# A gated linear attention and a feed-forward in one kernel: single chunks write their output transposed, by 32-column matmuls on quarters of the array

## The chip, the cores and the metric

The kernel runs on one core of a Trainium2 chip. The metric is the time on the device in microseconds (us), as the median of several runs. A profiled execution stands beside them; its span goes from the first to the last instruction.

## The reference

Two steps. A recurrent attention with a decay per feature (batch 4, 8 heads, 768 steps, head size 48), and then a feed-forward with a squared ReLU over all 3072 tokens (model width 384 = 8 x 48, inner width 2048):

```python
for t in range(S):
    state = alpha[:, :, t, :, None] * state + np.einsum('bhd,bhe->bhde', k[:, :, t], v[:, :, t])
    y[:, :, t] = np.einsum('bhd,bhde->bhe', q[:, :, t], state)
...
x = y.transpose(0, 2, 1, 3).reshape(B * S, H * D)
h = x @ w_in
r = np.maximum(h, 0.0)
g = r * r
return (g @ w_out).astype(np.float32)
```

## The kernel before

The recurrence is worked in chunks of 128 tokens, all 8 heads at once: 24 chunks (`NT`), 6 for each batch entry (`NCH`), so that chunks 0, 6, 12 and 18 begin a sequence and have no state to start from. Chunks 0 to 3 are worked as two "supers" of two chunks each (`add_super`); chunks 4 to 23 are "single" chunks (`add_chunk`, L401), of which 8 to 23 share the step of their scores in pairs (`PAIRS = 8`).

A single chunk goes through these steps:

- The logarithm of alpha on ScalarE (L411), its cumulative sum over the tokens as a matmul with a triangle (`e_p0`, L419), and the exponentials of the sum and of its negative (`e_A`, `e_Ai`, ScalarE). VectorE multiplies q and k by them (`e_qA`, L465, and `e_kI`, L472). GpSimd casts v to bf16 (`e_vb`, L414; the tile `vb`).
- TensorE transposes the scaled q and k, head pairs side by side in 128 rows with zeros as padding (`e_p1q`, `e_p1k`); a copy brings them to the tile `qkT` (`e_cp`).
- The scores k q^T of each head (`e_p2` in `add_scores`, L508): eight products a chunk on 64 of the 128 rows of the array, the two heads of a pair on different halves. VectorE masks them to the triangle (`e_sm`, L531; the tile `sm`, two halves `hh` of four heads each, called sm0 and sm1).
- The state: k^T v is added to `st` in PSUM (`e_ps`), VectorE decays it (`e_stm`), ScalarE copies it to bf16 (`e_sb`; the tile `sb`).
- The output (`add_back`, L545): y is the product of q with the state before the chunk (`e_p3a`, L576, four matmuls of 96 columns; a chunk that begins a sequence has none) plus the masked scores times v (`e_p3b`, L582, eight matmuls of 48 columns). The result has tokens on its rows.
- The tail (`add_tail`, L380): ScalarE copies y to the bf16 tile `xn`, TensorE transposes it in three parts (`e_p4`), and a copy on VectorE, or on ScalarE for early chunks, puts it into `xT_big` with features on the rows, as the feed-forward wants it.

The feed-forward runs over groups of chunks (4, 1, 1, and nine times 2): 16 tiles of the inner width times `w_in` (`add_moe1`), ReLU on ScalarE (L840), the square on VectorE (L848; the tile `gT`), and the product with `w_out` (`add_moe2`), whose result is copied to `ob` and stored.

The order of all instructions is laid out by a planner in the kernel's own code when the program is built (`Plan`, L61): each step is an `Op` with an engine (or several to choose from), a length, steps that it depends on, and a priority. Each engine then runs its instructions in exactly that order, and an instruction whose input is late holds up all that follow on its engine. Three of the planner's numbers bear on the change. `LEAD` (L330, used in `gate`) says how many chunks the cumulative sum of a chunk may be ahead of the feed-forward's progress. `PE_SLACK` and `PE_CALM` (L35, L36, used in `ready`) are the reserve that is planned between the end of another engine's step and the matmul that needs it: 0.05 us until the planned time of TensorE is at `PE_CALM`, and 0.25 us from there on. PSUM banks are slots, too: the attention's steps share two of them (`GLA_BANKS`), and a step that takes one gives it back when another step (`gives`) is done.

All matmuls are recorded under L254 (the helper `mm`), all transposes under L257, the copies of `cast` under L374 (ScalarE) and L376 (VectorE).

Of the kernel before, what the change touches and what calls it, by code (L numbers as in the profile page):

```python
# [8 lines left out]
FP32 = mybir.dt.float32  # L9
BF16 = mybir.dt.bfloat16  # L10
# [22 lines left out]

LAT = {"PE": 0.13, "ACT": 0.14, "DVE": 0.13, "POOL": 0.25}
PE_SLACK = 0.05  # L35
PE_CALM = 25.0  # L36
PAUSES = [(13.0, 1.0), (18.0, 1.0)]


# [17 lines left out]
def after(op, x=0.0):  # L57
    return (op, x)
# [88 lines left out]
def kernel(  # L147
# [10 lines left out]
    nc = tc.nc  # L158
    B, H, S, D = q.shape
    HD = H * D  # L160
    P = 128
    DP = 64
    NP = H // 2
    NCH = S // P
    d_model, d_ff = moe_w_in.shape
    n_tok = out.shape[0]
    KT = d_model // P
# [14 lines left out]
    big = ctx.enter_context(tc.tile_pool(name="big", bufs=1))  # L182
# [35 lines left out]
    for src, dst in ((utri_f, half_in), (sutri_f, half_ex)):  # L218
        nc.vector.memset(dst, 0.0)
        for ab in range(2):  # L220
            h = slice(ab * HF, ab * HF + HF)
            nc.vector.tensor_copy(dst[h, h], src[h, h])
    for ab in range(2):
        h = slice(ab * HF, ab * HF + HF)
# [10 lines left out]
    NBUF = 4  # L235
# [9 lines left out]
    nc.gpsimd.memset(kI_s[:, :, :, D:], 0.0)  # L245
    ae_s = big.tile([P, NBUF, 2, NP], FP32)
    nc.vector.memset(ae_s, 0.0)
    xT_big = big.tile([P, KT, n_tok], BF16)

    def pin(ins):  # L250
        tc.keep_in_program_order(ins)

    def mm(*a, **kw):
        pin(nc.tensor.matmul(*a, **kw))  # L254
# [4 lines left out]
    plan = Plan()  # L259
# [4 lines left out]
    GLA_BANKS = sl_bank[0:2]  # L264
# [4 lines left out]
    def psum(op, shape, dt):  # L269
        i = op.slot.bank  # L270
        return banks[i].tile(shape, dt, name=f"bank{i}")
# [6 lines left out]
    def add(eng, dur, emit, *deps, **kw):  # L278
        return plan.add(Op(eng, dur, emit, deps, **kw))
# [45 lines left out]
    C = [dict() for _ in range(NT)]  # L325
# [1 line left out]
    SRC = dict(srcs)  # L327
    EARLY = 2 * 3
    PAIRS = 8
    LEAD = 3.5  # L330

    NS = 2
    SIDE = 0
# [38 lines left out]
    def cast(op, out_t, in_t):  # L372
        if op.eng == "ACT":
            pin(nc.scalar.copy(out_t, in_t))  # L374
        elif op.eng == "DVE":
            pin(nc.vector.tensor_copy(out_t, in_t))  # L376
        else:
            pin(nc.gpsimd.tensor_copy(out_t, in_t))

    def add_tail(s, done, first, g):  # L380
        d = C[s]

        def e_xn():
            d["xn"] = work.tile([P, HD], BF16, name="xn")
            cast(xn, d["xn"], d["py"][:, 0:HD])
        xn = add("ACT", 0.36, e_xn, done, **g)
        first.gives = xn

        def e_p4():
            d["px"] = psum(p4, [P, KT, P], BF16)  # L390
            for j in range(KT):
                tr(d["px"][:, j, :], d["xn"][:, j * P:(j + 1) * P], ident_bf)
        p4 = plan.add(Op("PE", 0.165, e_p4, [xn], takes=GLA_BANKS, lat=0.14, **g))

        def e_xT():
            cast(xT, xT_big[:, :, s * P:(s + 1) * P], d["px"])
        xT = add({"ACT": 0.36, "DVE": 0.27} if s < EARLY else "DVE", 0.27, e_xT, p4, prio=-9.0)
        d["x"] = d["end"] = xT
        p4.gives = xT

    def add_chunk(s):  # L401
        d = C[s]
        b, c = divmod(s, NCH)
        i = s % NBUF
        L, qA, kI, ae = L_s[:, i], qA_s[:, i], kI_s[:, i], ae_s[:, i].rearrange("p j n -> p n j")
        old = C[s - NBUF].get("end") if s >= NBUF else None
        g = dict(prio=-10.0 + s * 0.01)
# [8 lines left out]
            pin(nc.gpsimd.tensor_copy(d["vb"], d["vt"]))  # L416
        vb = d["use_vt"] = add("POOL", 0.55, e_vb, d["ld_vt"], old, prio=-5.0)

        def e_p0():  # L419
            pm = d["pm"] = psum(p0, [P, 512], FP32)  # L420
            mm(pm[:, 0:HD], lhsT=utri_b[:, 0, :], rhs=L[:, :, 0:D], start=True, stop=True)
            for p in range(NP if s < TURN else 0):
                mm(pm[:, HD + p:HD + p + 1], lhsT=L[:, 2 * p:2 * p + 2, :], rhs=ones_col,
                   start=True, stop=True)
# [35 lines left out]
        else:  # L460
            p0.gives = ai
            ae1 = add("SPD", 0.4, e_aed, a_, lat=AE_LAT, **g)
# [12 lines left out]
        mk = d["use_kt"] = add("DVE", 0.47, e_kI, ai, d["ld_kt"], old, **g)  # L475
# [16 lines left out]
        if s < EARLY:  # L492
            cp = add({"ACT": 0.49, "DVE": 0.34}, 0, lambda: e_cp(0, NP), p1q, **g)
# [2 lines left out]
            cp = cpk = add("DVE", 0.61, lambda: e_cp(0, 2 * NP), p1k, **g)  # L496
        p1q.gives = cpk

        d.update(cps=[cp, cpk], mk=mk, vb_op=vb, ae1=ae1, kI=kI, ae=ae)
        if s < PAIRS:  # L500
            add_scores(s, 1)
            add_back(s)
        elif s % 2:
            add_scores(s - 1, 2)
            add_back(s - 1)
            add_back(s)

    def add_scores(s, n):  # L508
        pr = C[s:s + n]
# [32 lines left out]
        for hh, h in enumerate(hold):  # L542
            h.gives = pr[1]["sms"][hh]

    def add_back(s):  # L545
        d = C[s]
        b, c = divmod(s, NCH)
        g = dict(prio=-10.0 + s * 0.01)
        last = c == NCH - 1
        kI, ae, mk, vb, ae1 = d["kI"], d["ae"], d["mk"], d["vb_op"], d["ae1"]  # L550
        cp, (sm0, sm1) = d["cps"][0], d["sms"]

        if not last:
            def e_ps():
                if c == 0:
                    state["ps"] = ps_st.tile([P, NP, 2 * D], FP32, name="st")
                st = d["st"] = state["ps"]
                for p in range(NP):
                    mm(st[:, p, :], lhsT=kI[:, 2 * p:2 * p + 2, :], rhs=d["vb"][:, 2 * p:2 * p + 2, :],
                       start=(c == 0 and p == 0), stop=True, skip_group_check=True)  # L560
            prev = C[s - 1].get("sb") if s else None
            if c == 0 and s:
                prev = C[s - 2]["sb"]
            ps = plan.add(Op("PE", 0.17, e_ps, [mk, vb, ae1, prev], lat=0.16, **g))

            def e_stm():
                st4 = d["st"].rearrange("p n (j e) -> p n j e", j=2)
                pin(nc.vector.tensor_mul(st4, st4, bcast(ae, D)))  # L568
            stm = add("DVE", 0.47, e_stm, ps, ae1, prio=-2.0)

            def e_sb():
                d["sbt"] = work.tile([P, NP, 2 * D], BF16, name="sb")
                pin(nc.scalar.copy(d["sbt"], d["st"]))  # L573
            d["sb"] = add("ACT", 0.37, e_sb, stm, prio=-2.0)

        def e_p3a():  # L576
            d["py"] = psum(p3a, [P, 512], FP32)
            for p in range(NP):
                mm(d["py"][:, 2 * p * D:2 * (p + 1) * D], lhsT=d["qkT"][:, p, :], rhs=C[s - 1]["sbt"][:, p, :],
                   start=(p == 0), stop=False, skip_group_check=True)  # L580

        def e_p3b():  # L582
            if c == 0:
                d["py"] = psum(p3b, [P, 512], FP32)
            for hh in range(2):
                for p in range(NP):
                    h = 2 * p + hh
                    mm(d["py"][:, h * D:(h + 1) * D], lhsT=d["sm"][:, hh, p, :], rhs=d["vb"][:, h, :],
                       start=(c == 0 and hh == 0 and p == 0), stop=True, skip_group_check=True)
        p3a = None  # L590
        if c > 0:
            p3a = plan.add(Op("PE", 0.17, e_p3a, [cp, C[s - 1]["sb"], after(sm0)], takes=GLA_BANKS, **g))
        p3b = plan.add(Op("PE", 0.21, e_p3b, [after(sm1, 0.02), sm0, vb, after(p3a)], takes=None if c else GLA_BANKS, lat=0.15, **g))

        add_tail(s, p3b, p3a or p3b, g)

    def add_super(u):

# [424 lines left out]
```

## Time and profile before

| | us |
|---|---|
| median of 3 runs | 186.2 |
| lowest and highest of them | 185.51 and 186.7 |
| profiled execution | 185.78 |
| its span | 184.1 |

TensorE had the full clock granted throughout. The largest groups of the page, with the busy time of each (for matmuls, the mean of one includes the time through the array, and consecutive ones overlap):

| group | count | busy us | mean ns |
|---|---|---|---|
| TensorE, x times w_in, 256 columns | 480 | 61.1 | 273 |
| TensorE, g times w_out, 384 columns | 368 | 68.3 | 326 |
| TensorE, transposes of xn | 72 | 7.9 | 219 |
| TensorE, scores times v, 48 columns, single chunks | 160 | 7.4 | 183 |
| TensorE, q times state, 96 columns | 80 | 6.7 | 206 |
| ScalarE, ReLU | 96 | 56.1 | 602 |
| ScalarE, copy y to xn | 24 | 11.2 | 486 |
| VectorE, square | 96 | 42.8 | 470 |
| VectorE, mask of the scores, single chunks | 40 | 25.6 | 682 |
| VectorE, copy to xT_big | 19 | 6.7 | 354 |
| GpSimd, cast of v, single chunks | 20 | 10.8 | 542 |

How to read it: PE is TensorE, PEld its loads of weights, DVE is VectorE, ACT is ScalarE, POOL is GpSimd, SP is SyncE. In the page's name of a group, what stands before the arrow is written and what stands behind it is read; `64*128` means that 64 rows and 128 columns of the array were in use. The chain of waits is the work that ended last, followed back from the end.

### The profile page before, as it was taken

How to read it: one execution, taken by the hardware profiler on the slowest of the kernel's cores; microseconds unless marked ns; L12 is line 12 of the kernel's file. 1: busy time of each engine (PE TensorE's matmuls, PEld its weight loads, DVE VectorE, ACT ScalarE, POOL GpSimd, SP SyncE). 2: the span in 40 equal slices, each digit the busy share in tenths (PEclk: the TensorE clock that was granted, in tenths of full speed). 3: DMA queues.
4: the chain of work that ended last, by engine and by line, in shares of the span. 5: the costliest groups of instructions: out<-in, count | busy, mean ns of one | idle time of the engine just before them, and what ended most of it. 6: DMA issues, size and time to landing. Idle time of an engine off the chain costs nothing.

```text
span 184.1 us, 5041 instructions
## 1 busy us (share of the span) xinstructions
PE 178.6 (97%) x1992; PEld 133.4 (72%) x1993; DVE 134.8 (73%) x282; ACT 121.9 (66%) x259; POOL 27.6 (15%) x46
## 2 busy tenths in 40 slices
PE   7899999999999999999999999999999999999993
PEld 3567674666987788767867877777877878767763
DVE  6699669447998888856894997966996988852600
ACT  3565879267998598825939857847848768633721
POOL 6024476612011111111011011010010000000000
PEclk9999999999999999999999999999999999999999
DMA  5999999799898989893989899876701101012012
GB/s 139 276 281 323 318 341 375 156 222 212 168 215 174 220 158 214 180 217 84 205 197 209 202 206 201 192 148 149 187 0 43 46 2 48 0 45 89 0 43 85
DMA packets 101352, 30.23 MB, mean 164 GB/s; under 512 B 93776, under 2 KB 100560, under 8 KB 101328
## 3 DMA queue, kind: packets, MB, share of 16 engines
q1 hardware_dynamic: 101328, 29.91, 69.3%
q8 instruction: 15, 0.25, 0.5%
q14 instruction: 9, 0.07, 0.1%
HBM read 25.17 MB, written 4.72 MB: 162 GB/s over the span
## 4 chain that ended last, share of the span: by engine, by line
PE 90%; DVE 4%; DMA 2%; issue 1%; ACT 1%; DVEq 0%
PE bank L254 77%; PE bank L257 8%; DMA qt<-in_q_dram 2%; PE st L254 2%; PE sc L254 2%; DVE qkT L376 1%; DVE sm L726 1%; DVE sm L534 0%; DVE xT_big L376 0%; ACT r L840 0%; DVE qA_s L663 0%; DVE kI_s L663 0%; DVE qA_s L467 0%; ACT A L647 0%; DVE kI_s L473 0%
## 5 line engine op out<-in xcount | busy, mean ns | idle before, releaser
L254 PE MATMUL bank<-xT_big,w_in_b 128*128 128x256 bf16 (+2 forms) x599 | 73.3, 268 | 0.2
L254 PE MATMUL bank<-w_out_b,gT 128*128 128x384 bf16 (+2 forms) x400 | 70.9, 319 | 0.0
L840 ACT ACTIVATE r<-bank 128x512 bf16<-128x512 f32 x96 | 56.1, 602 | 16.1 <-PE bank L254 14.3
L254 PEld LDWEIGHTS <-w_in_b 128*128 128x128 bf16 x600 | 52.8, 98 | 9.3 <-issue 0.3
L848 DVE TENSOR_TENSOR gT<-r 128x512 bf16<-128x512 bf16 x96 | 42.8, 470 | 10.4 <-ACT r L840 10.1
L254 PEld LDWEIGHTS <-gT 128*128 128x128 bf16 x400 | 36.5, 98 | 18.4
L416 POOL CAST vb<-vt 128x384 bf16<-128x384 f32 x20 | 10.8, 542 | 92.0 <-PE bank L254 49.8
L376 DVE COPY qkT<-bank 128x1024 bf16<-128x1024 bf16 (+1 forms) x26 | 16.5, 646 | 4.8 <-PE bank L257 4.6
L912 ACT COPY ob<-bank 128x384 f32<-128x384 f32 x18 | 8.7, 483 | 16.1 <-PE bank L254 15.8
L534 DVE TENSOR_TENSOR sm<-sc,utri_b 128x512 bf16<-128x512 f32 x24 | 15.4, 683 | 3.0 <-PE sc L254 3.0
L374 ACT CAST xn<-bank 128x384 bf16<-128x384 f32 x24 | 11.2, 486 | 9.2 <-PE bank L254 9.1
L254 PEld LDWEIGHTS <-qkT 64*128 64x128 bf16 (+2 forms) x304 | 10.5, 97 | 5.6 <-issue 2.5
L376 DVE COPY xT_big<-bank 128x384 bf16<-128x384 bf16 x19 | 6.7, 354 | 10.5 <-PE bank L257 10.5
L470 DVE TENSOR_TENSOR qA_s<-qt,Af 128x384 bf16<-128x384 f32 x12 | 10.4, 869 | 2.5 <-ACT Af L439 2.5
L411 ACT ACTIVATE L_s<-at 128x384 bf16<-128x384 f32 x20 | 10.2, 523 | 2.1 <-DMA at<-in_alpha_dram 2.0
L439 ACT ACTIVATE Af<-bank 128x384 f32<-128x384 f32 x12 | 10.4, 865 | 1.6 <-ACT xn L374 1.0
L473 DVE TENSOR_TENSOR kI_s<-kt,Ainv 128x384 bf16<-128x384 f32 x20 | 11.3, 566 | 0.0
L443 ACT ACTIVATE Ainv<-bank 128x384 bf16<-128x384 f32 x20 | 10.3, 513 | 0.0
L534 DVE TENSOR_TENSOR sm<-bank,utri_b 128x512 bf16<-128x512 f32 x16 | 10.2, 681 | 0.0
L257 PE MATMUL bank<-ident_bf,qA_s 128*128 128x128 bf16 x96 | 9.5, 223 | 0.6 <-DVE qA_s L663 0.4
L254 PE MATMUL bank<-vb,sm 128*128 128x48 bf16 (+1 forms) x224 | 9.7, 183 | 0.0
L573 ACT CAST sb<-st 128x384 bf16<-128x384 f32 x16 | 7.7, 482 | 2.8 <-DVE st L568 2.6
(70 smaller groups left out, 174.2 us busy)
## 6 DMA issues: line engine op xcount, KB each, us to landing
at<-in_alpha_dram SPq DMA_DIRECT2D x24, 192.0 KB, 3.9
qt<-in_q_dram SPq DMA_DIRECT2D x24, 192.0 KB, 3.8
kt<-in_k_dram SPq DMA_DIRECT2D x24, 192.0 KB, 3.9
vt<-in_v_dram SPq DMA_DIRECT2D x20, 192.0 KB, 3.7
out_dram<-ob SPq DMA_DIRECT2D x19, 192.0 KB, 2.8
wo<-in_moe_w_out_dram SPq DMA_DIRECT2D x4, 768.0 KB, 7.7
wi<-in_moe_w_in_dram SPq DMA_DIRECT2D x4, 384.0 KB, 6.9
wi<-in_moe_w_in_dram SPq DMA_DIRECT2D x2, 768.0 KB, 5.8
```

Source lines behind the costliest of these rows:

```text
L254: pin(nc.tensor.matmul(*a, **kw))
L257: pin(nc.tensor.transpose(*a))
L374: pin(nc.scalar.copy(out_t, in_t))
L376: pin(nc.vector.tensor_copy(out_t, in_t))
L416: pin(nc.gpsimd.tensor_copy(d["vb"], d["vt"]))
L439: pin(nc.scalar.activation(d["A"], split(d["pm"][:, 0:HD], s), AF.Exp))
L443: pin(nc.scalar.activation(d["Ai"], d["pm"][:, 0:HD].rearrange("p (h d) -> p h d", h=H), AF.Exp, scale=-1.0))
L470: pin(nc.vector.tensor_mul(qA[:, :, 0:D].rearrange(v4, j=2), d["qt"].rearrange(v4, j=2), d["A"]))
L473: pin(nc.vector.tensor_mul(kI[:, :, 0:D], d["kt"], d["Ai"]))
L534: pin(nc.vector.tensor_mul(d["sm"][:, hh], d["sc"][hh], utri_b.to_broadcast([P, NP, P])))
L840: pin(nc.scalar.activation(box["r"][:, 0:w], box["ph"][:, 0:w], AF.Relu))
L848: pin(nc.vector.tensor_mul(gT[g][:, f0:f0 + per, lo * P:lo * P + n], r, r))
```

## The change

The output of single chunks is now computed with features on the rows from the start. `add_back` is split. `add_state` keeps the steps of the state. `add_y` replaces `e_p3a`, `e_p3b` and the tail: the state (32 of its columns) or v (32 columns) is the weight, and q or the masked scores, both 128 tokens wide, move. Each product thus gives 32 features of 128 tokens, in a quarter of the output's rows. A pair of heads has 96 features, that is 3 parts of 32 (`i`), and the four pairs 12 parts (`G`), which lie on the quarters `q = G % 4` in turn. The middle part of a pair belongs half to each head: for it v is taken from the new tile `vz`, which holds the 16 columns of the one head and zeros for the other, once for each head. GpSimd fills `vz` from `vb` (`e_vz`). So a chunk has 12 products with the state (none where it begins a sequence) and 16 with the scores. For pairs of chunks all this is one step of TensorE, which waits for everything that either chunk needs. One copy, on ScalarE or VectorE, takes the f32 result to `xT_big`; `xn` and its transposes are gone for these chunks, and the supers keep them. Besides, `LEAD` goes from 3.5 to 4.0 and `PE_CALM` from 25 to 60.

```diff
@@ -33,7 +33,7 @@
 
 LAT = {"PE": 0.13, "ACT": 0.14, "DVE": 0.13, "POOL": 0.25}
 PE_SLACK = 0.05
-PE_CALM = 25.0
+PE_CALM = 60.0
 PAUSES = [(13.0, 1.0), (18.0, 1.0)]
 
 
@@ -245,6 +245,8 @@
     nc.gpsimd.memset(kI_s[:, :, :, D:], 0.0)
     ae_s = big.tile([P, NBUF, 2, NP], FP32)
     nc.vector.memset(ae_s, 0.0)
+    vz_s = big.tile([P, NBUF, NP, 64], BF16)
+    nc.gpsimd.memset(vz_s, 0.0)
     xT_big = big.tile([P, KT, n_tok], BF16)
 
     def pin(ins):
@@ -327,7 +329,7 @@
     SRC = dict(srcs)
     EARLY = 2 * 3
     PAIRS = 8
-    LEAD = 3.5
+    LEAD = 4.0
 
     NS = 2
     SIDE = 0
@@ -416,6 +418,12 @@
             pin(nc.gpsimd.tensor_copy(d["vb"], d["vt"]))
         vb = d["use_vt"] = add("POOL", 0.55, e_vb, d["ld_vt"], old, prio=-5.0)
 
+        def e_vz():
+            mid = d["vb"].rearrange("p (n j) d -> p n (j d)", j=2)[:, :, 32:64]
+            pin(nc.gpsimd.tensor_copy(vz_s[:, i].rearrange("p n (a b) -> p n a b", b=16)[:, :, 0::3],
+                                      mid.rearrange("p n (a b) -> p n a b", b=16)))
+        vz = add("POOL", 0.3, e_vz, vb, old, prio=-5.0)
+
         def e_p0():
             pm = d["pm"] = psum(p0, [P, 512], FP32)
             mm(pm[:, 0:HD], lhsT=utri_b[:, 0, :], rhs=L[:, :, 0:D], start=True, stop=True)
@@ -496,14 +504,16 @@
             cp = cpk = add("DVE", 0.61, lambda: e_cp(0, 2 * NP), p1k, **g)
         p1q.gives = cpk
 
-        d.update(cps=[cp, cpk], mk=mk, vb_op=vb, ae1=ae1, kI=kI, ae=ae)
+        d.update(cps=[cp, cpk], mk=mk, vb_op=vb, vz_op=vz, vz=vz_s[:, i], ae1=ae1, kI=kI, ae=ae)
         if s < PAIRS:
             add_scores(s, 1)
-            add_back(s)
+            add_state(s)
+            add_y([s])
         elif s % 2:
             add_scores(s - 1, 2)
-            add_back(s - 1)
-            add_back(s)
+            add_state(s - 1)
+            add_state(s)
+            add_y([s - 1, s])
 
     def add_scores(s, n):
         pr = C[s:s + n]
@@ -542,13 +552,12 @@
         for hh, h in enumerate(hold):
             h.gives = pr[1]["sms"][hh]
 
-    def add_back(s):
+    def add_state(s):
         d = C[s]
         b, c = divmod(s, NCH)
         g = dict(prio=-10.0 + s * 0.01)
         last = c == NCH - 1
         kI, ae, mk, vb, ae1 = d["kI"], d["ae"], d["mk"], d["vb_op"], d["ae1"]
-        cp, (sm0, sm1) = d["cps"][0], d["sms"]
 
         if not last:
             def e_ps():
@@ -573,26 +582,56 @@
                 pin(nc.scalar.copy(d["sbt"], d["st"]))
             d["sb"] = add("ACT", 0.37, e_sb, stm, prio=-2.0)
 
-        def e_p3a():
-            d["py"] = psum(p3a, [P, 512], FP32)
-            for p in range(NP):
-                mm(d["py"][:, 2 * p * D:2 * (p + 1) * D], lhsT=d["qkT"][:, p, :], rhs=C[s - 1]["sbt"][:, p, :],
-                   start=(p == 0), stop=False, skip_group_check=True)
-
-        def e_p3b():
-            if c == 0:
-                d["py"] = psum(p3b, [P, 512], FP32)
-            for hh in range(2):
-                for p in range(NP):
-                    h = 2 * p + hh
-                    mm(d["py"][:, h * D:(h + 1) * D], lhsT=d["sm"][:, hh, p, :], rhs=d["vb"][:, h, :],
-                       start=(c == 0 and hh == 0 and p == 0), stop=True, skip_group_check=True)
-        p3a = None
-        if c > 0:
-            p3a = plan.add(Op("PE", 0.17, e_p3a, [cp, C[s - 1]["sb"], after(sm0)], takes=GLA_BANKS, **g))
-        p3b = plan.add(Op("PE", 0.21, e_p3b, [after(sm1, 0.02), sm0, vb, after(p3a)], takes=None if c else GLA_BANKS, lat=0.15, **g))
-
-        add_tail(s, p3b, p3a or p3b, g)
+    def y_groups(inter):
+        todo = [[] for _ in range(4)]
+        for G in range(3 * NP):
+            p, i = divmod(G, 3)
+            if inter:
+                todo[G % 4].append((G // 4, p, i, None))
+            else:
+                for hh in ((0,), (0, 1), (1,))[i]:
+                    todo[G % 4].append((G // 4, p, i, hh))
+        return [(q, *todo[q][n]) for n in range(len(todo[0])) for q in range(4)]
+
+    def add_y(chunks):
+        g = dict(prio=-10.0 + chunks[-1] * 0.01)
+        hold = []
+
+        def e_py(s, op):
+            C[s]["py"] = psum(op, [P, KT, P], FP32)
+
+        def e_y():
+            e_py(chunks[-1], y)
+            for s in chunks:
+                d, first = C[s], s % NCH > 0
+                for q, j, p, i, _ in y_groups(True) if first else ():
+                    mm(d["py"][32 * q:32 * q + 32, j, :], lhsT=C[s - 1]["sbt"][:, p, 32 * i:32 * i + 32],
+                       rhs=d["qkT"][:, p, :], start=(j == 0), stop=False, skip_group_check=True)
+                seen = set()
+                for q, j, p, i, hh in y_groups(False):
+                    if i == 1:
+                        v = d["vz"][:, p, 32 * hh:32 * hh + 32]
+                    else:
+                        v = d["vb"][:, 2 * p + hh, 16 * hh:16 * hh + 32]
+                    mm(d["py"][32 * q:32 * q + 32, j, :], lhsT=v, rhs=d["sm"][:, hh, p, :],
+                       start=(not first and q not in seen), stop=True, skip_group_check=True)
+                    seen.add(q)
+        deps = []
+        for s in chunks:
+            d = C[s]
+            deps += [*d["sms"], d["vz_op"], d["cps"][0]] + ([C[s - 1]["sb"]] if s % NCH else [])
+        for s in chunks[:-1]:
+            h = Op("NIL", 0.0, None, [C[chunks[-1]]["sms"][0], *hold], takes=GLA_BANKS, lat=0.0, **g)
+            h.emit = lambda s=s, h=h: e_py(s, h)
+            hold.append(plan.add(h))
+        dur = sum(0.41 if s % NCH else 0.24 for s in chunks) + 0.19
+        y = plan.add(Op("PE", dur, e_y, [*deps, *hold], takes=GLA_BANKS, lat=0.15, **g))
+        for s, op in zip(chunks, [*hold, y]):
+            d = C[s]
+
+            def e_xT(s=s, d=d):
+                cast(d["end"], xT_big[:, :, s * P:(s + 1) * P], d["py"])
+            d["x"] = d["end"] = op.gives = add({"ACT": 0.38, "DVE": 0.47}, 0, e_xT, y, prio=-9.0)
 
     def add_super(u):
 
```

## The prediction

> **What bounds the kernel now.** I read the page's busy shares first, then the chain of waits, then the timeline of TensorE, because the first two only name an engine. The busy line and the chain's sum by engine:
>
> ```profile
> PE 178.6 (97%) x1992; PEld 133.4 (72%) x1993; DVE 134.8 (73%) x282; ACT 121.9 (66%) x259; POOL 27.6 (15%) x46
> ...
> PE 90%; DVE 4%; DMA 2%; issue 1%; ACT 1%; DVEq 0%
> ```
>
> TensorE is the bound, and the other three have room over the whole span. A busy share hides pauses, though (the end of a matmul is modelled), so I went to the timeline of TensorE around chunks 8 and 9, the first pair (columns: start, length, engine, line, operation, output and inputs, shape, count):
>
> ```profile
> 62.29 0.49 PE L254 MATMUL bank<-xT_big,w_in_b 128*128 128x256 bf16 x3
> 62.72 0.40 PE L254 MATMUL sc<-qkT 64*128 64x128 bf16 x8
> 62.95 0.39 PE L254 MATMUL bank<-qkT 64*128 64x128 bf16 x8
> 63.27 2.47 PE L254 MATMUL bank<-xT_big,w_in_b 128*128 128x256 bf16 x21
> 65.57 0.33 PE L254 MATMUL bank<-sb,qkT 128*128 128x96 bf16 x4
> 65.74 0.36 PE L254 MATMUL bank<-vb,sm 128*128 128x48 bf16 x8
> 65.95 0.33 PE L254 MATMUL bank<-sb,qkT 128*128 128x96 bf16 x4
> 66.11 0.36 PE L254 MATMUL bank<-vb,sm 128*128 128x48 bf16 x8
> 66.32 0.81 PE L254 MATMUL bank<-xT_big,w_in_b 128*128 128x256 bf16 x6
> ...
> 67.68 0.33 PE L257 MATMUL bank<-ident_bf,xn 128*128 128x128 bf16 x3
> 67.85 1.15 PE L254 MATMUL bank<-xT_big,w_in_b 128*128 128x256 bf16 x9
> 68.83 0.33 PE L257 MATMUL bank<-ident_bf,xn 128*128 128x128 bf16 x3
> ```
>
> The reader is to take starts, not lengths: a group costs TensorE the time to the next start. The 21 matmuls from 63.27 to 65.57 go at 0.110 each, so the three at 62.29 are through at 62.62, yet the scores, which use half of the array's rows at a time, begin at 62.72: 0.10 to go into the split array. The 16 scores take 0.55 to 63.27. A full-array product of 128 columns costs 0.056 (three transposes, 67.68 to 67.85), so 8 pairs at 0.056 make 0.45 and 0.10 is left for going out. Compared in this way, start by start from 42 us on, the waits that are no such switch come to about 1.2 us (0.28 at 44.9, 0.19 at 52.3, 0.12 at 67.0, 0.25 at 69.7, 0.16 at 108.2, the rest under 0.06 each). So from there to the end the time is the sum of what TensorE has to do, and the change is worth what it does to that sum and to those waits.
>
> **What goes.** From the same rows: the first product with the state 65.57 to 65.74, 0.17; the eight with the scores 65.74 to 65.95, 0.21; a chunk's three transposes 0.17. A single chunk pays 0.55, a pair 65.57 to 66.32 and two times 0.17, 1.09; the first chunk of a sequence has no state product, 0.17 less. Chunks 4 to 7 are single (6 is a first chunk), 8 to 23 are eight pairs (12 and 18 are first). Sum: 3 x 0.55 + 0.38 + 6 x 1.09 + 2 x 0.92 = 10.4 us.
>
> **What comes.** 28 products of 32 weight columns and 128 moving columns a chunk (12 with the state, 16 with the scores; a first chunk 16 alone), each writing a quarter of the output rows, dealt out to the four quarters in turn. If four overlap, a chunk has 7 rounds, a first chunk 4: 3 x 7 + 4 + 6 x 14 + 2 x 11 = 131 rounds. No row of before has quarters by column. The nearest one has quarters of the other kind, 64 rows by 64 columns, in the opening chunks:
>
> ```profile
> 7.86 0.42 PE L254 MATMUL sc<-qkT 64*64 64x128 bf16 x16
> 8.21 0.28 PE L254 MATMUL bank<-warm 128*128 128x256 bf16 x1
> ```
>
> 16 products in 0.35: 4 rounds of 0.056 are 0.22, going out 0.10, 0.02 or 0.03 for a slow first round. So four quarters do overlap fully there, two of them on the same rows, each with its own weights. The rounds' bounds: 0.056 (this row) and 0.22 (four one after another at 0.056). I take 0.056, since the row is like the new one in size and number of parts and differs only in how the array is cut. Each of the 12 blocks (four singles, eight pairs) also goes in and out of the split array: 0.10 + 0.10 + 0.02 = 0.22, with 0 as the lower bound if a cut by columns alone needs no switch. Sum: 131 x 0.056 + 12 x 0.22 = 7.3 + 2.6 = 9.9 us. TensorE gains 10.4 - 9.9 = 0.5 us: singles lose 0.06 each, pairs gain about 0.09. It breaks even at 60 ns a round.
>
> At this place the Trainium skill, TensorE: Matmul & The Clock Gate, section "Measured speedup vs the span model", gives 2.38 times for three column tiles and 3.07 for four row tiles. By the latter a round would be an estimated 4/3.07 x 56 = 73 ns, 131 rounds 9.6 us, and the change a loss of 1.7 us instead of a gain of 0.5. The trace disagrees for a stream of rounds: four tiles above took what one takes.
>
> **The rest, step by step.** ScalarE loses 20 copies xn of 0.48 and in the order of the changed kernel gets 15 xT copies instead of 5 and 15 output copies instead of 18: 13 copies fewer, 6.2 us. VectorE goes from 19 xT copies of 0.35 and 5 output copies of 0.55 to 9 xT copies, now from f32 (the 0.55 of the output copies), and 8 output copies: 9.5 against 9.4 us. Nothing for the time, for neither is the bound. One of the two banks is held once per chunk instead of twice; TensorE waits for no bank in the view of waits, so nothing. GpSimd gets 20 copies of a third of vb: between 0.10 (its smallest memset) and 0.54 (the whole vb cast), taken as 0.3 by size, and one memset of twice the 0.53 ones, in its pause from 3.4 to 9.5 us. That pause hides it; without it the first vb cast would be 1.05 late.
>
> The new block waits for all scores of its chunks, the middle columns of v and the state at once, and everything on TensorE queues behind it. In the changed order at least 2.9 us of other matmuls stand between a pair's scores and its block (9 of 0.110 and 12 of 0.163 at the tightest); before, the four masks ended at 65.64, 2.4 after the scores. For the singles it is 1.75 (4 of 0.0425, the cumulative sums' 0.28, 8 of 0.163) against 1.4. Room of 0.5 and 0.35. The matmuls of a group come 1.3 us or more after its block (8 of 0.163); the copy of y needs 0.3 for the last products to end and start it and 0.55 to run. Covered by 0.45; the chain itself is shorter by xn, the transposes and one copy.
>
> LEAD lets a cumulative sum start 0.5 x 5.12 = 2.56 us of the feed-forward's work sooner. Its order on TensorE changes, no work. The loads of chunks 8 and 9 land at 50.94 and 54.86 and their sums began at 55.4 and 58.25, so the data is there. On SyncE's queue the same transfers are issued in nearly the same turn; the small ones of ae_s, for which that queue waited up to 8.8 us, move forward with the exponentials. PE_CALM takes 0.2 us of planned reserve out of the stretch from 25 to 60 us. Waits there were 0.6 of the 1.2 us; between none and double, I leave them as they are, since no row says which.
>
> **Forecast.** The profiled execution took 185.78 us (span 184.1 and 1.7 around it). It becomes 185.78 - 0.5 = 185.3; on the runs' median of 186.2 that is 185.7, and I say 185.6. With all 1.2 us of waits gone it is 184.4; with 1.2 more, 186.9.
>
> **Rivals.** *Quarters by column overlap only two at a time*, as the two halves of the scores' rows do (0.028 a product). Then 524 products x 0.028 + 2.6 = 17.3, 6.9 us more than before: 193. It decides from 60 ns a round on. For it: no row with four cuts on the same rows; against it, the 64 by 64 row. Chance 0.10.
>
> *Weights wait for the running product.* All 28 products use all rows, and if a load of weights could not run beside a product, each round would also pay an unhidden load, for which the 0.10 of a switch is the nearest price: 131 x 0.156 + 2.6 - 10.4 = +12.6, 198 to 199. Against it: the 128x48 products above come every 26 ns, each with its own 128x128 weights, and two of the 64 by 64 tiles share rows. Chance 0.03. The Trainium skill, the same page, section "What overlaps and what doesn't", says that weight loads overlap running matmuls only where the row groups differ; by that rule this rival is the outcome, and the trace speaks against it.
>
> *The block comes late.* VectorE slows beside GpSimd: a squaring that takes 0.41 to 0.47 elsewhere took 1.07 beside a cast there.
>
> ```profile
> 19.59 0.83 POOL L303 CAST w_in_b<-wi 128x768 bf16<-128x768 f32 x1 [1.29 <-DMA wi<-in_moe_w_in_dram]
> 19.62 1.07 DVE L848 TENSOR_TENSOR gT<-r 128x512 bf16<-128x512 bf16 x1
> ```
>
> If the 20 new copies hit the masks so that each chain is 0.6 late, the room of 0.35 to 0.5 is used up and the 12 blocks wait about 0.2 each, as much again before the feed-forward's first matmuls: +4 to 5 at most, half of it likely, 188.4. For it: VectorE is busy for 9.1 of the 10 us from 50 on. Chance 0.09.
>
> *No switch.* If a cut by columns alone neither enters nor leaves a mode, 12 x 0.2 = 2.4 us fall away: 183.2. Against it: every change of tile size in the trace shows the 0.10, from 64 by 64 to 64 by 128 too (16 scores from 10.66, the state products at 11.03). Chance 0.10, together with a vanishing of the waits.
>
> *Earlier chunks change nothing or everything*: if the loads held chunks back, LEAD would be without effect; that is inside the forecast.
>
> **Chances and range.** The forecast has 0.68, of which 0.03 each fall beyond 1% on either side through the waits. 1% is 1.9 us, about what a measurement tells here (the runs shown spread by 1.2). Faster by over 1%: 0.10 + 0.03 = 0.13; slower: 0.10 + 0.03 + 0.09 + 0.03 = 0.25; within 1%: 0.62. The range goes from 183.0, with the missing switch in, to 188.8, with the late block in, and leaves out the two rivals above 190, 0.13, and some edges.
>
> **What would show it.** In the changed profile: 12 blocks, a pair's taking about 1.0 us from the last full matmul to the next, rounds 56 ns apart; if they are 110 apart, the first rival, 150, the second. A pause of 0.10 on each side of a block, or none. Waits of TensorE for the masks or xT_big of more than 1.2 us in all would show the late block. The forecast is wrong if the rounds' pace is off by more than 12 ns or if the waits move by more than 1.5 us.

## The result and the profile after

The changed kernel takes 187.97 us (median of 9 runs, 186.69 to 190.87); the kernel before, run beside it, 186.2 (185.51 to 186.93). The ratio is 1.0092, 95% interval 1.0067 to 1.0117: slower by a little under 1%. The profiled execution took 187.53 us with a span of 185.8, 1.7 us more than the span of before. Medians, here and below, are over all executions; ratios leave out those that a lower clock or another disturbance made longer (three of these nine, 189.7 to 190.9, with a mean clock of 0.991).

The page's busy line and the chain's sum by engine, for the changed kernel:

```profile
PE 178.2 (96%) x2229; PEld 129.3 (70%) x2229; DVE 135.9 (73%) x275; ACT 117.5 (63%) x246; POOL 34.7 (19%) x67
...
PE 88%; DVE 5%; ACT 2%; issue 1%; DMA 1%; POOL 1%; SPq 0%; DVEq 0%; ACTq 0%; POOLq 0%
```

TensorE is still the bound, but its share of the chain fell from 90% to 88%; VectorE and ScalarE have 1% more each. ScalarE's 4.4 us less of work (the prediction reckoned with 6.2) won nothing by themselves. The measured time lies 2.4 us above the forecast of 185.6.

The timeline of TensorE around the block of chunks 8 and 9 (start, length, engine, line, operation, tiles, shape, count), of which the middle is left out:

```profile
65.98 2.11 PE L256 MATMUL bank<-w_out_b,gT 128*128 128x384 bf16 x12
68.02 0.35 PE L256 MATMUL bank<-qkT,sb 128*32 128x128 bf16 x12
68.20 0.22 PE L256 MATMUL bank<-sm,vb 128*32 128x128 bf16 x1
68.20 0.22 PE L256 MATMUL bank<-sm,vz_s 128*32 128x128 bf16 x1
68.21 0.22 PE L256 MATMUL bank<-sm,vb 128*32 128x128 bf16 x2
68.26 0.22 PE L256 MATMUL bank<-sm,vz_s 128*32 128x128 bf16 x2
...
68.77 0.22 PE L256 MATMUL bank<-sm,vb 128*32 128x128 bf16 x1
68.92 0.34 PE L256 MATMUL st<-vb,kI_s 128*128 128x96 bf16 x4
```

The 12 products before end their turn at 67.93 (0.163 each), so 0.09 goes into the switch. The first 12 products take 0.18, three rounds of four, 0.06 each; then four products start within 0.01 (68.20 to 68.21) and the next round at 68.26. The block costs 0.99 in all, and so do the other five pairs that begin no sequence. Before each of the 12 blocks stands the switch of 0.09 and no more: none waits for masks or values.

So the loss is elsewhere. The view of waits, VectorE's and TensorE's lines (waited in all, times, longest):

```profile
DVE st L577 <- DMA ae_s<-Af: 2.7, 1, 2.7
```

```profile
PE bank L256 <- DVE qkT L378: 2.0, 2, 1.8
PE bank L256 <- DVE both L217: 1.1, 1, 1.1
PE bank L256 <- ACT r L879: 0.6, 2, 0.4
```

In the trace of before VectorE's `st` waited for no transfer at all, and TensorE 0.2 for `qkT`. The timeline of VectorE shows where it is:

```profile
114.44 0.75 DVE L887 TENSOR_TENSOR gT<-r 128x512 bf16<-128x512 bf16 x2
117.93 0.57 DVE L577 TENSOR_TENSOR st<-st,ae_s 128x384 f32<-128x384 f32 x1 [2.74 <-DMA ae_s<-Af]
118.41 0.68 DVE L378 COPY qkT<-bank 128x1024 bf16<-128x1024 bf16 x1
```

VectorE stands for 2.74 us in front of the decay of the state (L577), which needs the decay factors `ae_s` of chunk 16. Behind it in VectorE's order is the copy of `qkT` for chunk 17, which has nothing to do with that state, but for which TensorE waits in the middle of a pair's scores:

```profile
116.95 0.40 PE L256 MATMUL sc<-qkT 64*128 64x128 bf16 x8
119.15 0.40 PE L256 MATMUL bank<-qkT 64*128 64x128 bf16 x8 [1.79 <-DVE qkT L378]
```

The last of the first eight starts at 117.14, 2.0 us before the next line. And this is the exponential on ScalarE that makes the decay factors of chunk 16 (`Af`), with SyncE's queue behind it (SPq):

```profile
109.30 0.86 ACT L447 ACTIVATE Af<-bank 128x384 f32<-128x384 f32 x1 [0.58 <-PE bank L256]
```

```profile
110.62 0.43 SPq L350 DMA_DIRECT2D at<-in_alpha_dram  x1
111.15 0.65 SPq L350 DMA_DIRECT2D qt<-in_q_dram  x1
111.90 0.78 SPq L350 DMA_DIRECT2D kt<-in_k_dram  x1
112.77 0.94 SPq L350 DMA_DIRECT2D vt<-in_v_dram  x1
113.76 0.94 SPq L350 DMA_DIRECT2D at<-in_alpha_dram  x1
114.79 1.42 SPq L464 DMA_DIRECT2D ae_s<-Af  x2
```

`Af` ended at 110.16. Its last row goes to `ae_s` by two transfers of 0.8 KB, and these are issued from 114.79 on, behind five loads of 192 KB that hold the queue for 0.4 to 0.9 us each (waits for a free tile included). The second one lands at 117.81, 7.65 us after `Af`. Before, the same transfers were issued 1.8 us after `Af`, landed after 4.4, and the decay did not wait:

```profile
111.10 0.86 ACT L439 ACTIVATE Af<-bank 128x384 f32<-128x384 f32 x1
```

```profile
112.66 1.01 SPq L348 DMA_DIRECT2D at<-in_alpha_dram  x1
113.77 1.28 SPq L456 DMA_DIRECT2D ae_s<-Af  x2
```

```profile
117.46 0.57 DVE L568 TENSOR_TENSOR st<-st,ae_s 128x384 f32<-128x384 f32 x1
```

So the exponential moved 1.8 us forward (from 111.96 to 110.16), while the queue came to its transfers 1.0 us later (from 113.77 to 114.79).

Start by start from 41.4 us on, as in the prediction, TensorE's work with its switches went from 137.93 to 137.71 us, its waits from 1.15 to 3.14. That makes 1.77 us more, and the span grew by 1.7.

### The profile page after: what moved, and what is told of

Same layout as the page of the kernel before. It is cut to its first block, busy times and chain, and to the rows that moved or that the text cites. A ratio compares the mean times of both kernels' runs of the same rounds, so it can differ in the third digit from the quotient of the medians.

```text
span 185.8 us, 5514 instructions
## 1 busy us (share of the span) xinstructions
PE 178.2 (96%) x2229; PEld 129.3 (70%) x2229; DVE 135.9 (73%) x275; ACT 117.5 (63%) x246; POOL 34.7 (19%) x67
## 4 chain that ended last, share of the span: by engine, by line
PE 88%; DVE 5%; ACT 2%; issue 1%; DMA 1%; POOL 1%; SPq 0%; DVEq 0%; ACTq 0%; POOLq 0%
PE bank L256 78%; PE bank L259 6%; PE st L256 2%; PE sc L256 2%; DVE qkT L378 1%; DVE sm L765 1%; DMA ae_s<-Af 1%; ACT r L879 1%; DVE half_in L222 1%; DVE st L577 1%; DVE half_ex L222 1%; ACT Af L447 0%; DVE qA_s L702 0%; DVE kI_s L702 0%; ACT A L686 0%
## 5 line engine op out<-in xcount | busy, mean ns | idle before, releaser
L879 ACT ACTIVATE r<-bank 128x512 bf16<-128x512 f32 x96 | 57.0, 600 | 19.7 <-PE bank L256 18.1
L256 PE MATMUL bank<-w_out_b,gT 128*128 128x384 bf16 (+2 forms) x400 | 69.4, 320 | 0.0
L256 PEld LDWEIGHTS <-gT 128*128 128x128 bf16 x400 | 37.3, 98 | 20.9 <-issue 0.3
L887 DVE TENSOR_TENSOR gT<-r 128x512 bf16<-128x512 bf16 x96 | 44.0, 485 | 10.4 <-ACT r L879 10.3
L418 POOL CAST vb<-vt 128x384 bf16<-128x384 f32 x20 | 10.2, 515 | 84.7 <-DMA vt<-in_v_dram 51.4
L951 ACT COPY ob<-bank 128x384 f32<-128x384 f32 x15 | 7.2, 480 | 13.3 <-PE bank L256 11.3
L577 DVE TENSOR_TENSOR st<-st,ae_s 128x384 f32<-128x384 f32 x16 | 8.9, 559 | 3.3 <-DMA ae_s<-Af 2.7
L256 PEld LDWEIGHTS <-qkT 64*128 64x128 bf16 (+2 forms) x236 | 6.2, 97 | 6.0 <-DVE qkT L378 3.4
L259 PE MATMUL bank<-ident_bf,kI_s 128*128 128x128 bf16 x96 | 9.3, 219 | 0.1
L376 ACT CAST xT_big<-bank 128x384 bf16<-128x384 f32 x12 | 5.8, 481 | 5.6 <-PE bank L256 5.5
(80 smaller groups left out, 185.6 us busy)
```

What stands on the lines that cost most here:

```text
L259: pin(nc.tensor.transpose(*a))
L879: pin(nc.scalar.activation(box["r"][:, 0:w], box["ph"][:, 0:w], AF.Relu))
L887: pin(nc.vector.tensor_mul(gT[g][:, f0:f0 + per, lo * P:lo * P + n], r, r))
```

## The experiments

The theory after this reading: the block itself is worth what was forecast, and the transfers of `ae_s`, late behind loads on SyncE's queue, take it back and more. Rivals: `LEAD` (more chunks under way, more loads in the queue), `PE_CALM`, or a cost of the block that the accounting misses.

**The parts one by one.** Of the changed kernel, one or both numbers set back; of the kernel before, both numbers changed.

```diff
-    LEAD = 4.0
+    LEAD = 3.5
```
(e1; e3 has this and the next)

```diff
-PE_CALM = 60.0
+PE_CALM = 25.0
```
(e2)

> The changed kernel with LEAD back at 3.5 and PE_CALM left at 60. Theory Q with LEAD as its cause (chunks that start sooner have their loads issued sooner, ahead of the decay factors): no wait for ae_s over 0.5 us, 185.3 to 186.3, ratio 0.995 to 1.001. Theory Q with PE_CALM as its cause: 187.3 to 188.5. Theory B: 187.3 to 188.5, with waits at the blocks.

> The changed kernel with PE_CALM back at 25 and LEAD left at 4.0. Its order from chunk 8 on is that of the changed kernel. Theory Q with LEAD as its cause: VectorE waits for ae_s about 2 to 3 us once, 187.3 to 188.5, ratio 1.006 to 1.012. Theory Q with PE_CALM as its cause: 185.3 to 186.3. Theory B: 187.3 to 188.5, with waits at the blocks.

> The changed kernel with both numbers of the planner put back (LEAD 3.5, PE_CALM 25): the new output blocks alone. Theory Q (queue: TensorE's work fell by 0.5 us as computed, and the loss is a wait of VectorE for a decay factor whose small transfer stands behind loads in SyncE's queue, brought about by the new order): 185.3 to 186.3 us, ratio 0.995 to 1.001, with the blocks' pace unchanged and no wait of VectorE for ae_s over 0.5 us. Theory B (the blocks themselves make things late, through all they wait for at once or through GpSimd's copies of v slowing VectorE): still slow, 187.3 to 188.5, ratio 1.006 to 1.012, with waits of TensorE right before the blocks or before the feed-forward's first matmuls behind them.

> The kernel before with the two numbers of the change alone (LEAD 4.0, PE_CALM 60), output as before. Theory Q: the numbers move the loads and the decay factors' transfers against each other, so some of the loss shows here, 186.5 to 188, ratio 1.002 to 1.01, through VectorE waiting for ae_s. Theory B: the numbers are harmless, 185.8 to 186.6, ratio 0.998 to 1.002.

| | median us | ratio to before, 95% |
|---|---|---|
| `LEAD` back (e1) | 186.45 | 0.998 (0.994 to 1.001) |
| `PE_CALM` back (e2) | 189.48 | 1.010 (1.006 to 1.014) |
| both back, the block alone (e3) | 188.75 | 1.010 (1.006 to 1.013) |
| kernel before with both numbers (e4) | 187.2 | 1.001 (0.997 to 1.005) |

The kernel before took 186.9 to 187.0 beside these and the next eight kernels, against 186.2 above. So a run is compared with the kernel before that ran beside it, by the ratio.

The numbers alone do nothing, and `LEAD` by itself is not the cause: with 3.5 the kernel is slow (e3) or not (e1), depending on `PE_CALM`. Each setting gives another order of the whole middle, and the waits go with it. In the view of waits, VectorE's decay in e3 and then in e1:

```profile
DVE st L577 <- DMA ae_s<-Af: 3.5, 2, 2.0
DVE st L577 <- PE bank L256: 1.8, 1, 1.8
```

```profile
DVE st L577 <- DMA ae_s<-Af: 1.4, 1, 1.4
```

In e3 three decays stand still for 1.5 to 2.0 us. The second line is the case in which a wait for several semaphores is put down to the wrong one: the decay starts at 92.10, and its transfer had landed at 91.98. TensorE's waits after 41.4 us are 5.3 us in e3, 1.0 in e1.

**Without the transfers.** The 24 transfers of `ae_s` of chunks 12 to 23 are left out, so that their states are decayed by what the buffer still holds (the factors of chunks 8 to 11, not zeros as the first expectation says); every other instruction stays, in the same order.

```diff
         def e_aed():
-            for j in range(2):
-                pin(nc.sync.dma_start(out=ae_s[HF * j:HF * j + D, i, j], in_=d["Af"][P - 1:P, j]))
+            pass
```

> The changed kernel without the small transfers that bring the decay factors of chunks 12 to 23 to ae_s (the factors stay at zero, so these chunks' states are left out); every other instruction and the order on the other four engines is the same. Theory Q (the loss is VectorE's wait for these transfers, as the traces of the changed kernel and of the blocks alone show at the decay of the state): the 2.7 us wait and TensorE's 2.0 behind it are gone, 185.0 to 186.2 us, ratio 0.993 to 1.000. Rival D (SyncE's queue as such, or the loads, run late, and the decay factors are only the first to be hit): another wait takes the place, 187 to 188.5, ratio 1.004 to 1.012.

> The kernel before without the same transfers. Both theories: its decays waited for almost nothing (0.3 us once), so 185.6 to 186.6, ratio 0.996 to 1.002. With the run of the changed kernel without them beside it, it gives what the blocks are worth when that wait is out of the way: theory Q says the changed one is 0.2 to 0.8 us faster than this.

> The new blocks with both planner numbers of before, without the transfers of the decay factors. Its trace with them had VectorE wait three times for ae_s (1.8, 2.0 and 1.5 us) and TensorE lose 5.3 us in all. Theory Q: TensorE's waits fall to about 1 to 1.5 us, 185.0 to 186.2, ratio 0.993 to 1.000. Rival D: 187 to 189.

Measured: the changed kernel 185.4, ratio 0.995 (0.992 to 0.998); the kernel before 185.76, 0.995 (0.992 to 0.998); the block alone 185.34, 0.993 (0.990 to 0.995). So without the transfers all three take the same within 0.4 us, and nothing is left of the loss: it lies in these transfers. Leaving them out also frees 24 turns of SyncE's queue; that the loss comes through the decay is what the wait of 2.7 us in the trace shows. The kernel before gained 0.5% as well, though in its trace no decay waits for a transfer, and in e13 below it gains nothing; what that 0.5% is stays open. In n3 TensorE's view of waits has nothing from the middle left over 0.3 us:

```profile
PE bank L256 <- DVE both L217: 1.1, 1, 1.1
PE bank L259 <- DVE qA_s L701: 0.3, 1, 0.3
PE bank L256 <- ACT r L878: 0.2, 1, 0.2
```

**Other places for the transfers.** Three ways to get them out from behind the loads. First, the loads of later chunks are emitted 3 us later than planned (e7 from chunk 15 on, e9 from chunk 17 on):

```diff
-        self.order.sort(key=lambda o: o.start)
+        self.order.sort(key=lambda o: o.start + getattr(o, "later", 0.0))
...
+        d["ld_" + nm].later = 3.0 if s > TURN + 2 else 0.0
```

> The changed kernel with the loads of chunks 15 and later put 3 us further back in the order of SyncE's queue alone, so that the decay factors and the stores come ahead of two or three loads each; the order on the other engines is the same, nothing is left out. Theory Q: the factors land before VectorE asks for them, or wait under 0.5 us, 185.0 to 186.3, ratio 0.993 to 1.000. Rival D: the loads are late in their turn, and ScalarE, GpSimd or VectorE wait for at, qt, kt or vt instead, 187 to 189.

> The changed kernel with the loads of chunks 17 and later alone put 3 us back in SyncE's order. With chunks 15 and 16 moved as well, the wait for ae_s went and the logarithm of a chunk waited 3 us for alpha at 85 us in its place, after which TensorE ran at half its pace for some 3 us. Theory Q: with that one spared, 185.2 to 186.5 us, ratio 0.993 to 1.000. Rival D: a load of a later chunk becomes late instead, 187 to 189.

e7 took 189.56 (1.014, 1.009 to 1.018), e9 187.3 (1.003, 0.999 to 1.006). In e7 no decay waits for a transfer any more; a load of `at` is late instead. ScalarE's timeline:

```profile
83.29 0.60 ACT L880 ACTIVATE r<-bank 128x512 bf16<-128x512 f32 x1 [1.98 <-PE bank L256]
86.89 0.52 ACT L414 ACTIVATE L_s<-at 128x384 bf16<-128x384 f32 x1 [3.00 <-DMA at<-in_alpha_dram]
```

The ReLUs behind that logarithm hold TensorE for 2.6 us. Loads and small transfers compete for turns on one queue: here the one gained what the other lost.

Second, ScalarE's own queue, in the changed kernel (e6) and in the one before (e10):

```diff
-                pin(nc.sync.dma_start(out=ae_s[HF * j:HF * j + D, i, j], in_=d["Af"][P - 1:P, j]))
+                pin(nc.scalar.dma_start(out=ae_s[HF * j:HF * j + D, i, j], in_=d["Af"][P - 1:P, j]))
```

> The changed kernel with the decay factors' transfers issued from ScalarE's queue instead of SyncE's; the planned order is the same and nothing is left out. Theory Q: the transfers go out right after the exponential that makes them, VectorE does not wait for ae_s, 185.2 to 186.5 us, ratio 0.993 to 1.000, unless the issues hold ScalarE up (24 of them, 0.6 us each on SyncE's queue; then ReLU comes late and some of it is given back). Rival D (everything behind SyncE is late): 187 to 189.

> The kernel before with the decay factors' transfers issued from ScalarE's queue, as a control for the changed kernel with the same edit. Theory Q: little to gain, 185.6 to 186.6, ratio 0.996 to 1.002; the changed kernel with this edit is 0.2 to 0.8 us faster than this one. Rival D: 185.8 to 187.5, no faster than the changed kernel's.

191.2 (1.024, 1.020 to 1.028) and 189.74 (1.016, 1.012 to 1.020). The decays wait no more, but ScalarE stands still while it issues, and its ReLU comes late. TensorE's waits in e6:

```profile
PE bank L256 <- ACT r L879: 2.9, 6, 0.7
PE bank L256 <- DVE both L217: 1.1, 1, 1.1
PE bank L259 <- ACT Ainv L451: 0.9, 3, 0.5
```

Third, the planner is told that a transfer takes 8 us instead of 4 (`AE_LAT = 8.0`, e5), so that decays are planned later.

> The changed kernel with the planner told that a decay factor lands 8 us after its issue instead of 4 (AE_LAT). VectorE's decay of the state is then planned later, behind other work; the order of chunks 12 to 23 changes throughout. Theory Q: no wait for ae_s over 0.5 us, TensorE's waits 1 to 1.5 us, 185.2 to 186.5 us, ratio 0.993 to 1.001. Rival D: 187 to 189.

It took 189.06 as a median, with a ratio of 1.003 (0.999 to 1.007). The two disagree, so this settles nothing; in its profiled execution one decay still waits 3.9 us for its transfer.

**GpSimd's queue.** GpSimd issues none of the loads and stores and is busy 19% of the span. The same edit with `nc.gpsimd`, in the changed kernel (e12) and in the one before (e13); and as a test of what makes SyncE's queue late, the changed kernel with the loads of v from chunk 12 on issued there (e15), since one of them waited for a copy on GpSimd until 113.63.

```diff
-            pin(nc.sync.dma_start(out=d[nm], in_=SRC[nm][b, c]))
+            pin((nc.gpsimd if nm == "vt" and s >= TURN else nc.sync).dma_start(out=d[nm], in_=SRC[nm][b, c]))
```
(e15)

> The changed kernel with the 24 small transfers of ae_s issued from GpSimd's queue, which has nothing else to issue and is busy 19% of the span. Theory (the small transfers stand behind loads on SyncE's queue, and the vector engine's decay of the state waits for them): they land within about 4 us of Af, VectorE's idle time before st stays under 1 us each, TensorE's waits after 42 us fall from 3.1 to about 1 and the time is 185.4 to 186.2, ratio to the kernel before 0.995 to 1.000. Rival (the transfer itself is slow, by the 16 DMA engines' load, whatever queue issues it): decays wait as before, 187.5 to 188.5. Second rival: GpSimd is held by the issue or runs its casts of v first, so that the transfers come later still: 188 to 190.

> The kernel before with its ae_s transfers issued from GpSimd's queue. By the theory of SyncE's queue it gains what it still loses to them: leaving them out took 0.5%, so 185.5 to 186.3, ratio 0.996 to 1.000. If GpSimd's queue costs something of its own, it shows here too: 187 or more.

> The changed kernel with the v loads of chunks 12 to 23 issued from GpSimd's queue instead of SyncE's: that queue loses 12 of its transfers of 192 KB, and with them the waits for GpSimd's reads of vt (0.89 us before the one at 113.6). If it is the waiting v loads that make SyncE's queue late, the ae_s transfers of chunk 16 land about 1 to 2 us sooner and the time is 185.5 to 186.8, ratio under 1.002. If the queue is late through its sheer number of transfers, some of it: 187. If GpSimd's issue of such a load costs its casts time, 188 or more.

| | median us | ratio to before, 95% |
|---|---|---|
| changed, `ae_s` on GpSimd's queue (e12) | 185.54 | 0.998 (0.995 to 1.000) |
| before, the same (e13) | 185.68 | 1.000 (0.998 to 1.001) |
| changed, v loads on GpSimd's queue (e15) | 188.23 | 1.014 (1.010 to 1.018) |
| kernel before beside them | 185.76 | |

e12 is the changed kernel with its loss gone; TensorE's waits after 41.4 us are 0.9 us. The changed kernel without this edit did not run beside it: its 0.9% is from the result above, and the nearest beside it is e15, 1.4%, whose transfers stay on SyncE's queue. GpSimd's timeline, and VectorE's at the place where it stood before:

```profile
110.32 0.99 POOL L464 DMA_DIRECT2D ae_s<-Af  x2 [1.63 <-ACT Af L447]
112.45 0.99 POOL L464 DMA_DIRECT2D ae_s<-Af  x2 [1.14 <-ACT Af L447]
```

```profile
114.03 0.76 DVE L887 TENSOR_TENSOR gT<-r 128x512 bf16<-128x512 bf16 x2
115.08 0.57 DVE L577 TENSOR_TENSOR st<-st,ae_s 128x384 f32<-128x384 f32 x1 [0.28 <-PE st L256]
115.55 0.68 DVE L378 COPY qkT<-bank 128x1024 bf16<-128x1024 bf16 x1
```

The first transfer of each pair is issued 0.29 us after `Af`, and the decay waits for its matmul alone. Over the 24 transfers, from the tile view of `ae_s` and the ends of `Af`:

| | before | after | e12 |
|---|---|---|---|
| from the end of `Af` to the issue, mean us | 1.30 | 1.83 | 0.54 |
| from the issue to landing, mean us | 2.18 | 2.60 | 2.70 |
| both, mean and longest us | 3.48, 5.48 | 4.44, 8.05 | 3.24, 4.85 |

From issue to landing the means are much alike; the place in the queue is what differs. The planner reckons with 4.5 us from the end of `Af` (0.14 until the next step can start, 0.4 for the issue, 4 to land): before, the longest went over it by 0.9, after by 3.5. In the plan these transfers never stand behind a load, either: they have an engine of their own there (`SPD`), and the loads another. The plan keeps 0.5 us of the loads' time for a pair, which takes SyncE 1.2 (two of 0.58). e15 went against its theory: without the v loads VectorE's wait is as long (2.8; `ae_s` of chunk 16 lands 7.5 us after `Af`), so the v loads are not what makes the queue late.

## Why the prediction was wrong

- **What bounds the kernel, and the price of the block: right.** Rounds of four are 56 ns apart and each block goes in and out for the 0.1 on either side. The 12 blocks cost TensorE 9.91 us, counted in the same way; forecast 9.9. The first two rivals (two quarters at a time; weights that wait for the running product) and the missing switch fall with it. The Trainium skill, TensorE: Matmul & The Clock Gate, "What overlaps and what doesn't", would have loads of weights overlap only between different row groups. The trace disagrees: all 28 products of a chunk use all rows, each with its own weights, and their rounds go at 56 ns, the pace of one full product.
- **The gain of 0.5 us: of the right kind, rather smaller.** Before rounding, the prediction's rows give 0.43 (10.41 less 9.98), and the traces bear that out: the old steps, counted start to start in the trace of before, take 10.3 us, the new blocks 9.9. TensorE's work and switches as a whole fell by only 0.2 after 41.4 us; where the other 0.2 went, the traces do not show in any one place. With the transfers left out the two kernels' ratios are alike (0.995 both) and their medians 0.4 apart; with the transfers on GpSimd's queue they are 0.1 apart. So of the time the gain is between 0 and 0.4.
- **The failed step: SyncE's queue.** "On SyncE's queue the same transfers are issued in nearly the same turn; the small ones of ae_s, for which that queue waited up to 8.8 us, move forward with the exponentials." Their turn was nearly the same, but the queue itself ran late: the exponentials of chunks 15 to 17 came 1.8 to 3.2 us earlier, the issues behind them between 0.9 us earlier and 1.0 later. Its waits of up to 8.8 us in the trace of before were read as room for the whole span, but the longest came at chunks 20 and 22; at chunks 13 to 17 it was already 1.6 to 2.8 us behind. In the changed order it came to 4.6 behind at chunk 16 and 5.3 at chunk 17, and the 4.5 us that the planner allows were used up: VectorE waited 2.7 us for the factors of chunk 16, and TensorE 1.8 behind it. The price shows in e12: with only these transfers moved, the ratio is 0.998 instead of 1.009.
- **Waits "between none and double, I leave them as they are".** They went to 3.14, beyond the double of 1.2, and by more than the 1.5 us that the prediction names as its sign of being wrong. The value taken had no mechanism behind it, and the mechanism was to be found in the trace of before, which shows the small transfers landing up to 5.5 us after `Af` against the 4.5 planned.
- **The block comes late: wrong.** Masks and values of v were there for every block. Its 188.4, and the upper end of the range that was drawn to take it in, lie near the measured time by luck.
- **`LEAD` and `PE_CALM` without price of their own: right** (e4), but each shuffles the order, and with the block the shuffles range from 0.998 to 1.010 (e1, e2, e3).

Open is why the orders with the block load SyncE's queue less evenly. e15 excludes the v loads as the cause. More buffers for the loaded tiles, which would let loads go out earlier, were not tried.

The best version is the changed kernel with `ae_s` on GpSimd's queue (e12): 0.2% under the kernel before, with an interval that ends just below 1 (0.9999), so hardly a gain. With `LEAD` set back (e1) the ratio is the same, with an interval on both sides of 1.

## What to carry to other kernels

When a change reorders a planned schedule, take each queue's lateness in the trace of before (end of the producer to issue, issue to landing, beside the latency that the planner assumes) as a term of the sum: the smallest margin there is what the new order can use up. A transfer of a few hundred bytes that a chain depends on does not belong on a queue that issues large loads in order; give it a queue of an engine with time to spare, and see what that engine's own work loses (here the kernel became 1.6 to 2.4% slower than before with ScalarE's queue, and no slower with GpSimd's). And in an in-order engine the price of a late input is paid by whatever stands behind it: here a copy that did not need the decay.

## What the runs showed of the hardware

A pause of TensorE can cost more than itself. In e7, after the wait of 2.6 us at 85.2, the granted clock went to half. The windows view (stretch, length, busy time of PE, PEld, DVE, ACT, POOL, then PEclk, share of DMA, GB/s), and TensorE's timeline:

```profile
82.00:85.00 3.00, 3.00 (x34) 2.65 (x33) 1.59 (x3) 0.60 (x1) 0.80 (x2) 1.00 0.56 131
88.20:91.20 3.00, 3.00 (x18) 2.20 (x17) 2.15 (x5) 2.63 (x6) 0.00 (x0) 0.50 0.12 24
92.00:95.00 3.00, 3.00 (x42) 2.21 (x39) 2.47 (x5) 1.94 (x4) 0.00 (x0) 1.00 0.68 136
```

```profile
87.95 2.72 PE L256 MATMUL bank<-xT_big,w_in_b 128*128 128x256 bf16 x12 [2.40 <-ACT r L880]
90.46 0.63 PE L259 MATMUL bank<-ident_bf,qA_s 128*128 128x128 bf16 x4
```

The 12 products take 2.51 us to the next start, 0.21 each instead of 0.11, and the half clock lasts from 87.9 to 91.3: about 1.6 us lost on top of the 2.6. A wait of 2.0 us did this in the profiled execution of e2 (from 120.1; half the clock from 123.3 to 126.7) but not in that of the changed kernel.

The clock records of the traces show why. In e2, e5 and e7 the half clock lasts 3.41 us each time, and it begins a whole number of such spans (35, 38 and 24) after the full clock was granted. If each trace is cut into spans of 3.41 us on that grid, TensorE was idle for 1.79, 2.32 and 2.40 us of the span just before the half clock. In no other span between 20 and 175 us, in any of the 17 traces, was it idle for more than 1.76 us, and all of these were followed by the full clock. The wait of e2 fell into one span; that of the changed kernel was cut by a border of the grid, into 1.67 and 0.12. The windows view, the changed kernel first, then e2:

```profile
115.62:119.03 3.41, 1.73 (x19) 1.04 (x17) 1.10 (x3) 1.09 (x3) 0.00 (x0) 1.00 0.78 149
119.03:122.45 3.42, 3.30 (x29) 2.23 (x30) 3.42 (x9) 1.08 (x2) 0.00 (x0) 1.00 0.81 175
```

```profile
119.88:123.29 3.41, 1.62 (x25) 1.15 (x25) 2.37 (x6) 0.98 (x2) 0.00 (x0) 1.00 0.74 151
123.29:126.71 3.42, 3.42 (x12) 1.64 (x11) 2.98 (x6) 0.60 (x1) 0.00 (x0) 0.50 0.69 141
```

So it is the idle time within such a span that counts, with the limit between 1.76 and 1.79 us in these traces, and a pause of 2 us costs more than itself or not by where it falls. One half-clock span makes a mean clock of 0.991 over 188 us (an estimate: half of 3.41 is lost). The Trainium skill, TensorE: Matmul & The Clock Gate, "What's actually happening", gives an idle window of about 3.4 us that runs freely, whatever the kernel does. The traces agree on its length and on its running freely, but the window does not have to be idle throughout: 1.79 us of it were enough here.

Issuing a transfer of 0.8 KB took 0.50 us on GpSimd's queue and 0.58 on SyncE's (the middle one of 24 each). The loads of 192 KB in the queue's rows above took 0.4 to 0.9. So on this queue a small transfer costs about as much of a turn as a large one.
